# One wait fewer between the input loads of two pairs, in a fused Mamba-2 scan and bilinear FFN

## The chip, the cores and the metric

The kernel runs on 1 core of one Trainium2 chip. The metric is the device time of one execution in microseconds (us). The kernel before was run five times: 131.21, 131.57, 132.05, 132.27 and 133.94 us, median 132.05. One of these, of 131.57 us, was profiled; the profile's span is 129.80 us, so 1.77 us of that execution lie outside the span.

## What is computed

The first half is a chunked state-space scan (Mamba-2, SSD form) with 4 batches, 8 heads, 768 positions, head size 32 and state size 16. The second half is a bilinear feed-forward layer over the 3072 tokens, with d_model 256 and d_ff 1536:

```python
cum = np.cumsum(log_a[chunk]); L = np.exp(cum_i - cum_j) * causal
y_intra = ((C @ B.T) * L) @ x
y_inter = (C @ state) * exp(cum)
state = exp(sum(log_a)) * state + sum_j exp(cum_last - cum_j) * outer(B_j, x_j)
y = y_intra + y_inter                       # [batch, head, seq, 32]
X = y.transpose(0, 2, 1, 3).reshape(3072, 256)
out = ((X @ w_a) * (X @ w_b)) @ w_out       # [3072, 256], float32
```

## The kernel before

**Tiling.** The kernel cuts the 768 positions into 6 blocks of 128. Two batches are handled together as a "pair", so there are 12 pairs, numbered p = 2 * block + half. For each pair it loads B, C and x of two batches into three tiles `bn`, `cn`, `xn` (line 113), each with three buffers. A load (`load1`, line 119) takes one of the three inputs of one of the two batches, so a pair has six loads. Those of B and C move 64 KB each in pieces of 128 bytes (two positions of 16 float32), those of x 128 KB in pieces of 256 bytes. Below, "B 2/1" means the load of B for pair 2, batch 1 of the two.

**What a pair does.** POOL (for pair 0: DVE) scales B and C by factors of the decay (`scale_bc`, line 251: `bm`, `cm`). TensorE transposes both (line 306), ACT and DVE move them out of PSUM (lines 315, 316), TensorE makes the scores (line 329), DVE, and POOL for one of the four parts, mask them (lines 360, 362), ACT or POOL makes a float16 x (lines 247, 249), and TensorE multiplies (lines 371, 388, 405). ACT moves the result to `X2T` (line 417). From pair 4 on the transposes are DMAs (line 285). The feed-forward layer of a pair is six `unit`s of 16 matmuls (line 470), each with an ACT copy (479) and a DVE product (480), and two `out_half`s of 12 matmuls (line 487). Unit k2 needs `Wa` and `Wb` of third k2 // 2.

**Order.** It is written out by hand under `manual_schedule`: every engine runs its instructions in program order. TensorE has, from line 572 on: units (0,0) and (0,1), the decay factors, the transposes of pair 1, unit (0,2), scores of pair 1, units (0,3) and (0,4), `pv(1)`, units (0,5), (1,0), (1,1), (1,2), then line 612, the transposes of pair 2, then unit (1,3). So nothing after line 612 can run on TensorE before `bm` and `cm` of pair 2 are there.

**Queues.** SP issues most loads, ACT the loads of batch 1 of pair 0 and the small constant `c32`; both are hardware-described DMAs. The weights go through POOL's queue, which also casts them to float16: Wa and Wb of third 0, Wa of third 1 before the scan (lines 190, 197), Wb of third 1 and both of third 2 at lines 551 and 552, `Wo` at line 555. An SP instruction that has to wait holds everything behind it on SP.

**Completion semaphores.** The recording layer hands out eight completion semaphores in turn to the DMAs of SP and ACT, in program order, and a DMA waits for the one that had its semaphore before it. So at most eight such DMAs are in flight, and each load waits for the landing of the eighth load before it. This is seen in the built program's list of instructions with their waits:

| load | waits for the landing of |
|---|---|
| B 1/0 (line 142) | x 0/1 (the explicit wait, line 143) and B 0/1 |
| C 1/1, B 1/1, C 1/0 | a, C 0/1, B 0/0 |
| x 1/0, x 1/1 | C 0/0, x 0/0 |
| B 2/0, B 2/1 | x 0/1, c32 |
| C 2/0, C 2/1 | B 1/0, C 1/1 |
| x 2/0, x 2/1 | B 1/1, C 1/0 |
| B 3/0 (line 557) | x 1/0, Wb of third 2 (line 558), DVE's use of the old buffer |

Of the kernel before, what the change touches and what calls it, by code (L numbers as in the profile page):

```python
# [15 lines left out]
AFTER = mybir.DependencyInfo(mybir.DependencyClass.Sync, mybir.DependencyReason.DATA)  # L16
# [6 lines left out]
def kernel(  # L23
# [14 lines left out]
    nc = tc.nc  # L38
# [80 lines left out]
    def load1(eng, p, which, bt):  # L119
        blk, bp = divmod(p, NBP)  # L120
        src = (B, C, x)[which][2 * bp + bt, :, blk * Q : (blk + 1) * Q, :]
        return eng.dma_start(  # L122
            pair_in[p][which][64 * bt : 64 * bt + 64].rearrange("i h r n -> i h (r n)"),
            src.rearrange("h (i r) n -> i h (r n)", r=2),
        )
# [10 lines left out]
    load1(nc.scalar, 0, 1, 1)  # L136
    load1(nc.sync, 0, 1, 0)
    nc.scalar.preload_act_table_set("natural_log_exp_and_others")
    x_in = load1(nc.scalar, 0, 2, 1)
    nc.scalar.dma_start(c32, p32_t.ap())  # L140
    load1(nc.sync, 0, 2, 0)
    b_in = load1(nc.sync, 1, 0, 0)
    tc.add_manual_dep(b_in.ins, x_in.ins.name, AFTER, reason="inputs of pair 0 first")
    load1(nc.sync, 1, 1, 1)
    load1(nc.sync, 1, 0, 1)
    load1(nc.sync, 1, 1, 0)
# [572 lines left out]
```

## Time and profile before

| what | us |
|---|---|
| median of 5 runs | 132.05 |
| the profiled execution | 131.57 |
| its span | 129.80 |
| TensorE busy (93% of the span) | 121.3 |
| DVE, ACT, POOL busy | 87.3, 66.5, 58.7 |
| SP's one wait for x 0/1, ending at 7.04 | 3.7 |
| busy share of the 16 DMA engines from 5 to 8, 8 to 9.25 | 1.22, 1.24 |
| from 9.25 to 11.5, from 11.5 to 12.75 | 1.06, 0.67 |
| from 12.75 to 19.25, 19.25 to 24.3, 24.3 to 26 | 1.31, 1.42, 0.40 |

Times inside the execution are counted from the start of the span. A DMA has an issue (the time of its instruction on SP, ACT or POOL) and a landing: in the trace each of the 16 DMA engines posts one completion, and the load has landed with the last of them. The busy share of the DMA engines goes over 1 where packets of two queues overlap on an engine. Some loads, from the trace of before:

| load | issue | landing |
|---|---|---|
| C 0/0, x 0/0 (SP) | 2.04, 2.71 | 6.20, 8.91 |
| C 0/1, x 0/1, c32 (ACT) | 1.56, 2.27, 2.98 | 4.82, 7.02, 8.74 |
| B 1/0, C 1/1, B 1/1, C 1/0 | 7.10, 7.74, 8.42, 9.10 | 11.47, 11.75, 12.07, 12.39 |
| x 1/0, x 1/1 | 9.85, 10.83 | 13.45, 16.85 |
| B 2/0, B 2/1 | 11.50, 12.18 | 19.62, 21.21 |
| C 2/0, C 2/1 | 13.06, 13.81 | 22.71, 24.27 |
| x 2/0 (x 2/1 next) | 16.30 | 24.58 (25.42) |
| Wa, Wb of third 0 | 2.27, 3.21 | 8.07, 9.56 |
| Wa, Wb of third 1 | 5.17, 10.26 | 10.94, 14.99 |
| Wa, Wb of third 2 | 11.02, 11.73 | 17.81, 19.25 |
| Wo | 13.87 | 24.02 |

### The profile page before, as it was taken

What the parts mean: (1) busy time and instruction counts of PE and PEld (TensorE: products, weight loads), DVE (VectorE), ACT (ScalarE), POOL (GpSimd) and SP (SyncE); (2) the same over time, 40 slices, a digit from 0 to 9 for tenths busy, and PEclk for the clock granted to TensorE, in tenths of its full rate; (3) what the DMA queues carried; (4) which work ended last, traced back from release to release, by engine and by line L of the source; (5) the groups of instructions that cost most, each with busy time, mean ns of one, the idle gap of its engine ahead of it and who ended that gap; (6) DMA issues with size and microseconds to landing.
All of it is one profiled execution on the core that took longest, in us unless ns stands there. A gap on an engine that the chain in (4) does not pass through costs nothing.

```text
span 129.8 us, 4697 instructions
## 1 busy us (share of the span) xinstructions
PE 121.3 (93%) x1921; PEld 99.5 (77%) x1921; DVE 87.3 (67%) x167; ACT 66.5 (51%) x129; POOL 58.7 (45%) x90
## 2 busy tenths in 40 slices
PE   6899979699999999999999999999999999999960
PEld 2345857588888888888888988888888889888840
DVE  4475769748494976975967939949849649464420
ACT  3243484495846544546455555456365454574410
POOL 7719730489961934909518529249058000000000
PEclk9999999999999999999999999999999999999999
DMA  3998999774536556655957466564656210111203
GB/s 64 154 216 142 207 204 204 126 140 74 144 71 110 129 99 116 134 92 116 107 85 157 88 103 140 103 126 95 106 105 135 57 44 5 40 40 25 45 15 81
DMA packets 51557, 13.79 MB, mean 106 GB/s; under 512 B 45328, under 2 KB 51504, under 8 KB 51536
## 3 DMA queue, kind: packets, MB, share of 16 engines
q1 hardware_dynamic: 46560, 10.72, 44.5%
q0 software_dynamic: 3184, 2.36, 11.9%
q10 hardware_dynamic: 1792, 0.41, 1.6%
q8 instruction: 15, 0.25, 0.9%
q14 instruction: 6, 0.05, 0.2%
HBM read 11.13 MB, written 3.15 MB: 110 GB/s over the span
## 4 chain that ended last, share of the span: by engine, by line
PE 77%; DMA 12%; SPq 5%; ACTq 1%; issue 1%; POOL 1%; DVE 0%; POOLq 0%; ACT 0%
PE ops L487 25%; PE aps L470 22%; PE bps L470 21%; DMA cn<-in_C_dram 8%; SPq L122 5%; DMA xn<-in_x_dram 4%; PE SC L329 3%; PE SC L371 3%; PE SC L405 2%; ACTq L122 1%; PE SC L388 1%; POOL bm L255 0%; PE SC L306 0%; DVE osb L500 0%; POOL cm L255 0%
## 5 line engine op out<-in xcount | busy, mean ns | idle before, releaser
L480 DVE TENSOR_TENSOR hk<-bps,asb 128x512 f16<-128x512 f32 x72 | 49.2, 688 | 22.9 <-ACT asb L479 21.0
L479 ACT COPY asb<-aps 128x512 f32<-128x512 f32 x72 | 42.2, 587 | 17.6 <-PE aps L470 16.0
L470 PE MATMUL aps<-X2T,Wa 128*128 128x256 f16 x288 | 43.5, 273 | 0.0
L470 PE MATMUL bps<-X2T,Wb 128*128 128x256 f16 x288 | 43.2, 273 | 0.4 <-DMA Wb<-in_moe_w_b_dram 0.4
L487 PE MATMUL ops<-Wo,hk 128*128 128x256 f16 x288 | 35.3, 273 | 0.0
L470 PEld LDWEIGHTS <-Wb 128*128 128x128 f16 x288 | 28.1, 98 | 3.9 <-DMA Wb<-in_moe_w_b_dram 0.6
L362 DVE TENSOR_TENSOR t<-SC,causal 128x512 f16<-128x512 f32 x45 | 29.4, 682 | 1.5 <-ACT tmp L359 0.9
L487 PEld LDWEIGHTS <-hk 128*128 128x128 f16 x288 | 27.5, 98 | 3.5
L470 PEld LDWEIGHTS <-Wa 128*128 128x128 f16 x288 | 26.8, 98 | 4.3 <-DVE X2T L429 0.3
L445 POOL TENSOR_TENSOR sbd<-U,maskbd 128x512 f16<-128x512 f32 x10 | 11.6, 1158 | 26.3 <-PE ops L487 15.1
L502 ACT ACTIVATE osb<-ops 128x256 f32<-128x256 f32 x23 | 8.8, 384 | 23.3 <-PE ops L487 21.2
L249 POOL TENSOR_SCALAR x<-xn 128x512 f16<-128x512 f32 x9 | 13.4, 1491 | 1.0 <-DMA xn<-in_x_dram 0.3
L417 ACT ACTIVATE X2T<-SC 128x512 f16<-128x512 f32 x11 | 6.6, 597 | 7.4 <-PE SC L388 6.4
L441 DVE SCALAR_TENSOR_TENSOR U<-SC,G,gU 128x64 f32<-128x64 f32 x16 | 3.8, 280 | 6.1 <-ACT X2T L417 6.1
L255 POOL TENSOR_TENSOR bm<-bn,fB 128x256 f16<-128x256 f32 x11 | 6.9, 629 | 0.0
L201 PE MATMUL SC<-warm 128*128 128x512 f16 (+1 forms) x14 | 5.1, 516 | 1.2 <-DVE warm L150 1.2
L360 POOL TENSOR_TENSOR t<-tmp,causal 128x512 f16<-128x512 f32 x3 | 3.5, 1155 | 6.2 <-ACT tmp L359 6.2
L273 POOL TENSOR_TENSOR bc<-bn,fB 128x128 f16<-128x128 f32 x16 | 6.2, 408 | 0.0
L269 POOL TENSOR_TENSOR bc<-cn,fC 128x256 f16<-128x256 f32 x8 | 5.0, 623 | 1.7 <-DMA cn<-in_C_dram 1.0
L201 PEld LDWEIGHTS <-warm 128*128 128x128 f16 x23 | 2.5, 130 | 4.1 <-issue 2.7
L371 PE MATMUL SC<-t,x 64*32 64x128 f16 x352 | 4.8, 218 | 0.2 <-DVE t L362 0.2
L371 PEld LDWEIGHTS <-x 64*32 64x32 f16 x384 | 3.2, 91 | 2.3 <-issue 1.2
(68 smaller groups left out, 68.1 us busy)
## 6 DMA issues: line engine op xcount, KB each, us to landing
xn<-in_x_dram SPq DMA_DIRECT2D x23, 128.0 KB, 3.9
out_dram<-osb SPq DMA_DIRECT2D x46, 64.0 KB, 2.1
bn<-in_B_dram SPq DMA_DIRECT2D x23, 64.0 KB, 3.1
cn<-in_C_dram SPq DMA_DIRECT2D x23, 64.0 KB, 3.5
Wa<-in_moe_w_a_dram POOLq DMA_DIRECT2D x3, 256.0 KB, 5.8
Wb<-in_moe_w_b_dram POOLq DMA_DIRECT2D x3, 256.0 KB, 6.4
Wo<-in_moe_w_out_dram POOLq DMA_DIRECT2D x1, 768.0 KB, 10.1
xn<-in_x_dram ACTq DMA_DIRECT2D x1, 128.0 KB
```

The lines of the kernel that those rows point to most:

```text
L122: return eng.dma_start(pair_in[p][which][64 * bt : 64 * bt + 64].rearrange("i h r n -> i h (r n)"), src.rearrange("h (i r) n -> i h (r n)" ...
L201: nc.tensor.matmul(bank[:, 0:cols], warm[:, 0:128], warm[:, 0:cols], start=True, stop=True, skip_group_check=True)
L249: eng.tensor_scalar(xo, xi, XS, None, ALU.mult)
L255: eng.tensor_tensor(out=m_, in0=pair_in[p][which].rearrange("p h r n -> p r h n"), in1=f[:, blk, :, bp].unsqueeze(3).broadcast_to((128, 2, ...
L362: nc.vector.tensor_tensor(out=o_, in0=i_, in1=c_, op=ALU.mult)
L371: nc.tensor.matmul(py[bt][32 * g : 32 * g + 32, u * Q : (u + 1) * Q], s["X16"][k, h, r, :], s["T1"][k, h, r, :], start=(first and u == 0 a ...
L445: nc.gpsimd.tensor_tensor(out=Sbd.rearrange("p t (m c) -> p t m c", m=4), in0=U32[:, p].unsqueeze(2).broadcast_to((128, 2, 4, 2 * D)), in1 ...
L470: nc.tensor.matmul(ps[:, kk * 2 * Q : (kk + 1) * 2 * Q], W[:, f, k * 128 : (k + 1) * 128], X2T[:, p, f].rearrange("p t q -> p (t q)"), sta ...
L479: nc.scalar.copy(asb, a_ps)
L480: return lambda: nc.vector.tensor_tensor(out=s["hk"][:, 2 * k2 : 2 * k2 + 2, :].rearrange("p k q -> p (k q)"), in0=b_ps, in1=asb, op=ALU.mult)
L487: nc.tensor.matmul(o_ps[:, 0:d_model], hk[:, k, bt * Q : (bt + 1) * Q], Wo[:, k, :], start=(k == 0), stop=(k == NK - 1), skip_group_check= ...
L502: nc.scalar.activation(out=o_sb, in_=o_ps[:, 0:d_model], func=AF.Copy, scale=1.0 / (YS * YS))
```

## The change

```diff
-    x_in = load1(nc.scalar, 0, 2, 1)
+    load1(nc.scalar, 0, 2, 1)
     nc.scalar.dma_start(c32, p32_t.ap())
     load1(nc.sync, 0, 2, 0)
-    b_in = load1(nc.sync, 1, 0, 0)
-    tc.add_manual_dep(b_in.ins, x_in.ins.name, AFTER, reason="inputs of pair 0 first")
+    load1(nc.sync, 1, 0, 0)
     load1(nc.sync, 1, 1, 1)
```

The explicit wait of SP for the landing of x 0/1 ahead of B 1/0 is gone. No instruction is added, removed or put in another place on any engine. In the built program one more thing is different: B 1/0 now takes the eighth completion semaphore, which no DMA had before it, and `c32` on ACT takes the first one, so that B 1/0 waits for nothing and `c32` waits for the landing of B 0/1. Accordingly B 2/1 waits for B 1/0 (before: c32), C 2/0 for c32 (before: B 1/0), and B 2/0 carries the wait for x 0/1 itself. All other waits of the table stand.

## Prediction

> **What bounds the kernel now.** I read the page's engine table first, then the chain of waits, then TensorE's waits in the start-up, then the timeline around the longest of them, then the DMA queues by window.
>
> ```profile
> PE 121.3 (93%) x1921; PEld 99.5 (77%) x1921; DVE 87.3 (67%) x167; ACT 66.5 (51%) x129; POOL 58.7 (45%) x90
> ...
> DMA  3998999774536556655957466564656210111203
> ...
> PE 77%; DMA 12%; SPq 5%; ACTq 1%; issue 1%; POOL 1%; DVE 0%; POOLq 0%; ACT 0%
> ```
>
> TensorE is the bound: in the windows from 26 to 113 us it is busy 87.00 of 87.00. The other 12% DMA and 5% SP in the chain are all in the first 25 us, where the row of DMA tenths is at 9. A us gained or lost on TensorE before 26 is thus a us of the span; one gained on any other engine is nothing until TensorE feels it. The chain, asked for 12 to 27 us, shows where it enters TensorE:
>
> ```profile
> 13.81 10.45 DMA cn<-in_C_dram
> 24.27 0.02 issue
> ...
> 24.98 0.63 POOL bm L255
> 25.61 0.05 issue
> 25.65 0.40 PE SC L306 x4
> ```
>
> The load C 2/1, issued at 13.81, takes 10.45 us; POOL then makes `cm` and `bm`; only then can TensorE transpose pair 2. TensorE's own waits from 10 to 27 us price it, beside all others:
>
> ```profile
> PE SC L306 <- POOL bm L255: 1.2, 1, 1.2
> PE SC L329 <- DVE ct L316: 0.4, 1, 0.4
> PE bps L470 <- DMA Wb<-in_moe_w_b_dram: 0.4, 1, 0.4
> PE SC L371 <- DVE t L362: 0.2, 1, 0.2
> ```
>
> The timeline gives the two that inputs and weights cause to the hundredth:
>
> ```profile
> 19.30 0.61 PE L470 MATMUL bps<-X2T,Wb 128*128 128x256 f16 x4 [0.37 <-DMA Wb<-in_moe_w_b_dram]
> ...
> 24.40 0.62 POOL L255 TENSOR_TENSOR cm<-cn,fC 128x256 f16<-128x256 f32 x1 [5.39 <-DMA cn<-in_C_dram]
> ...
> 25.65 0.28 PE L306 MATMUL SC<-ident,bm 128*128 128x128 f16 x2 [1.18 <-POOL bm L255]
> ```
>
> So 1.18 us hang on pair 2's C, and 0.37 on Wb of third 2. POOL was free for `cm` from 19.0 on (5.39 us idle): there is nothing else ahead of it. The removed wait itself is 3.7 us long but on SP, not on TensorE:
>
> ```profile
> SPq L122 <- DMA xn<-in_x_dram: 3.7, 1, 3.7
> ```
>
> **What the Trainium skill says.** "DMA: Bandwidth & Descriptors", section "Issuing engines are not separate DMA queues": DMAs of SP, ACT and POOL end on the same 16 engines and interleave. The trace agrees: from 13.75 to 19.25 POOL's queue (q0) takes 94.8% and SP's (q1) 38.4%. Its section "Queues, rings and completion order": on an engine each queue is consumed in ring order, and queues with work take turns packet by packet. The trace fits: x 0/0 came ahead of everything later on SP, and no queue shuts another out. Its section "Why a DMA increments its semaphore by 16 and not by 1": only the full 16 mean landed. Here C 2/1's first completion is at 21.51, its last at 24.27; the slowest engine decides.
>
> **The change part by part.**
>
> *SP's issues.* x 0/0's issue ends at 3.35. B 1/0 can follow at 3.40 (before 7.10: 3.70 earlier). Each issue takes about 0.63 with 0.05 to the next. The remaining semaphore waits then hold: C 1/1 at 4.05, B 1/1 at 4.82 (landing of C 0/1), C 1/0 at 5.5, x 1/0 at 6.25 (C 0/0 landed at 6.20), x 1/1 at 8.95 (x 0/0 landed at 8.91; before 10.83). B 2/0 follows at 9.63 (before 11.50), and pair 2 comes 1.9 us earlier all along if its own waits (landings of B 1/0, c32, C 1/1) are met by then. So of 3.70 us pair 2 keeps 1.9: the wait for x moves from x 0/1 (7.02) to x 0/0 (8.91).
>
> *From issue to landing.* The DMA engines decide what that is worth. By window:
>
> ```profile
> 8.00:9.25 1.25, 1.25 (x27) 0.50 (x12) 0.83 (x2) 0.84 (x2) 0.09 (x1) 1.00 1.24 205
> 9.25:11.50 2.25, 2.23 (x39) 0.83 (x37) 1.06 (x2) 0.78 (x4) 2.25 (x3) 1.00 1.06 166
> 11.50:12.75 1.25, 1.21 (x11) 0.82 (x10) 1.15 (x4) 0.53 (x2) 1.17 (x3) 1.00 0.67 117
> 12.75:19.25 6.50, 5.80 (x108) 4.53 (x105) 4.51 (x13) 4.38 (x11) 3.76 (x5) 1.00 1.31 205
> ```
>
> The last two columns are the DMA share and GB/s. From 8 to 9.25 the engines are full of weights alone (266 packets of q0, none of q1), from 9.25 to 11.5 of pair 1's B and C (2065 packets of q1, 130 of q0). Exchanging these two in time gains nothing: 396 weight packets at 266 per 1.25 us are 1.86 us, 2065 of q1 at their fastest (325 in a quarter us) 1.6, together 3.5, the whole stretch. The room is from 11.5 to 12.75, at half load: there x 1/0 runs alone, x 1/1 begins only at 13.75, after Wb of third 1 has taken the engines. With both x waiting in the ring, they follow at 11.5; at the pace of 14.0 to 14.5 (330 packets) a load of 512 takes 0.75 us, so x 1/1 starts near 12.25 and not at 13.75: 1.5 us earlier. Behind it the queue is unchanged, so I move C 2/1's landing by the same 1.5, to 22.8. Bounds: nothing (24.27) if the engines' total work sets it; 1.9 (22.4) if the issue does; refilling only the idle share, 1.25 * (1.31 - 0.67) / 1.31 = 0.6, gives 23.7.
>
> *On TensorE.* From C 2/1's landing to the transpose are 25.65 - 24.27 = 1.38 us. TensorE is ready at 24.48, so a landing up to 23.10 removes the whole 1.18 us; at 22.8 there are 0.3 to spare, at 23.7 only 0.6 us are gained.
>
> *Weights.* Pair 1's and 2's earlier packets now share engines with weights. Wb of third 0 (landed 9.56, used at 12.29) and Wa of third 1 (10.94, used at 15.24) have 2.7 and 4.3 us of cover. Wb of third 1 (14.99, used at 15.67) has 0.68, Wa of third 2 (17.81, used at 18.32) 0.51, Wb of third 2 none. New contention is from 12.75 to 13.75, where q1 was nearly empty. In the window 11.5 to 13.75 and in that from 19.25 to 24.3, q0 keeps some 80% beside a full q1 (81.1% in the latter against 94.8%): 20% of 1 to 1.5 us is 0.2 to 0.3 us later. On Wb of third 2 the first 0.20 is hidden by the wait for DVE's mask at 20.34, so 0.1 us is charged. Bounds: 0, or the full issue advance of 3.7 on the weights.
>
> *Pair 0.* x 0/0 and the loads before it are ahead of B 1/0 in the same ring, and x 0/1's packets end at 6.25, before the first of x 0/0's: nothing of pair 1 can run before 8.0. c32 now waits for B 0/1 (landed 3.38): issue 3.42 for 2.98. Behind it on ACT is the copy at 5.07, and it is first read at 14.96. Nothing. Without that cover an x 0/0 later by over 0.6 us would hold pair 0's products (scaled x ends at 9.57, used at 10.25).
>
> *Late next.* With TensorE 1.1 us earlier, x 2/1 (landed 25.42) is read near 27.6, C 3/1 (27.25) near 28.9; DVE's product at 24.70 ends at 25.39, ahead of its banks' reuse by unit (1,4) near 25.8. None binds.
>
> Sum: 129.80 - 1.18 + 0.1 = 128.7 for the span, plus 1.77 outside: 130.5 against 131.57. The median of five is 0.48 above that execution, so from it: 132.05 - 1.08 = 131.0.
>
> **Rivals.** *Hidden anyway.* The engines are full from 5 to 24, and SP's issues themselves stretch there (C 2/1's takes 2.44 us): the earlier issue only waits longer, C 2/1 lands at 24 or later: 131.8 to 132.2. Against it stands the half-empty window. *Both stalls go.* If the filled window also brings Wb of third 2 forward by 0.4, 1.18 + 0.37 give 130.5; half the further wait for DVE, 130.3. *Weights late (slower).* At 19.30 TensorE waits for Wb of third 2; if the weights lose the 3.7 us that SP's queue wins, Wb lands at 22.95, TensorE loses 3.65 and gets back 1.18: 132.05 + 2.5 = 134.5. It decides from a landing after 20.43 us (1.18 late) on. For it: no slack on that load. Against: turn-taking leaves q0 80%. *No earlier issue.* The eight semaphores could put another wait in the wait's place; the built program shows B 1/0 with none, so I give that none by itself.
>
> **Chances.** Forecast 0.5 (130.5 to 131.6), hidden 0.22, both stalls 0.15, weights late 0.13. About 1% is what a measurement of this kernel can tell from no change: below 130.73 is the whole of "both stalls" and a quarter of the forecast's case, 0.27; above 133.37 most of "weights late", 0.11; the rest 0.62. The range takes all of "both stalls" except its lowest end, the forecast, "hidden", and the start of "weights late": 130.2 to 132.8; the forecast's own is 130.5 to 131.6.
>
> **What would show it.** Right: SP's issue of B 1/0 near 3.4 and of B 2/0 near 9.6; the DMA share from 11.5 to 12.75 over 1; C 2/1 landed before 23.1; no wait of line 306 for POOL; Wb's wait under 0.6. Wrong: C 2/1 again after 24, a wait at line 470 for Wb over 1 us, or ACT waiting for x 0/0 after 9.5.

## The result, and the profile after the change

The changed kernel takes 130.13 us in the median of 41 executions (129.04 to 132.30), the kernel before 131.63 us in 78 (129.99 to 137.57). The ratio is 0.9917 with a 95% interval of 0.9897 to 0.9936. It compares, for each kernel, only the executions within 1.5% of its fastest, which leaves out the long ones (15 of the 78 before took over 133 us, none of the 41 after), so the medians lie further apart, by 1.1%. The profiled execution took 129.55 us with a span of 127.85.

The page after, at the places shown of before (engine table, DMA tenths, chain):

```profile
PE 119.4 (93%) x1921; PEld 98.7 (77%) x1921; DVE 88.3 (69%) x167; ACT 66.6 (52%) x129; POOL 58.7 (46%) x90
...
DMA  3999999875356556555856464574565210111203
...
PE 84%; DMA 8%; DVE 2%; SPq 1%; POOL 1%; issue 0%; ACT 0%; DVEq 0%; POOLq 0%
```

SP's share of the chain fell from 5% to 1%. SP's timeline after (columns: start, length, instruction) shows the wait gone and what is left of the head start:

```profile
3.40 0.64 SPq L122 DMA_DIRECT2D bn<-in_B_dram  x1
4.07 0.63 SPq L122 DMA_DIRECT2D cn<-in_C_dram  x1
4.88 0.64 SPq L122 DMA_DIRECT2D bn<-in_B_dram  x1
5.57 1.67 SPq L122 DMA_DIRECT2D cn<-in_C_dram  x1
7.28 2.62 SPq L122 DMA_DIRECT2D xn<-in_x_dram  x2
9.95 1.60 SPq L122 DMA_DIRECT2D bn<-in_B_dram  x2
```

The windows after (last columns: DMA share and GB/s) have 1.26 from 11.5 to 12.75, where the profile before had 0.67:

```profile
9.25:11.50 2.25, 2.19 (x30) 1.40 (x29) 1.32 (x6) 1.12 (x4) 2.18 (x4) 1.00 1.39 217
11.50:12.75 1.25, 1.25 (x24) 0.98 (x22) 1.22 (x4) 0.75 (x2) 0.00 (x0) 1.00 1.26 149
```

In bytes the rise is smaller, from 117 to 149 GB/s. The share adds up the time of every packet, and it goes over 1 with one queue alone too (1.24 from 8 to 9.25 before, where only weights moved), so packets and bytes tell more. From 8 to 11.5 us, for SP's loads (q1) and the weights (q0), in packets, MB and share, they are before:

```profile
q0 software_dynamic: 396, 0.37, 64.9%
q1 hardware_dynamic: 2065, 0.26, 47.7%
```

and after:

```profile
q1 hardware_dynamic: 2482, 0.36, 70.2%
q0 software_dynamic: 407, 0.38, 67.6%
```

TensorE's waits after, 10 to 27 us:

```profile
PE SC L305 <- POOL bm L254: 0.6, 1, 0.6
PE bps L469 <- DMA Wb<-in_moe_w_b_dram: 0.5, 2, 0.4
PE SC L370 <- DVE t L361: 0.4, 1, 0.4
```

All lines have moved up by one. The first of these is not the wait of before: it stands at 14.22, at the transposes of pair 1 (C 1/0 landed at 12.82). Those of pair 2 start at 23.65 without a wait. C 2/1 landed at 19.77 (24.27 before), x 1/1 at 15.58 (16.85).

Two stages of the two executions differ. TensorE's first unit begins at 10.23 (11.64 before): pair 0 started earlier, with C 0/0 landed at 5.57 (6.20). From the first unit to the transposes of pair 2 it took 13.41 us (14.02). From there to the end it is 104.20 (104.19). So 1.40 of the 2.00 us are in pair 0's start, all but the end of which lies ahead of the first packet of a moved load (7.64), and only 0.61 in the stretch where I expected the win. This split is no division of causes, though. Before, the transposes of pair 2 came 1.38 us behind C 2/1's landing (24.27, 25.65), as they did in all other profiles that waited for this load (1.38 or 1.39). With that landing given, an earlier first unit would only have made the wait longer.

### The profile page after: what moved, and what is told of

It reads as the page before. It is cut to its first block, busy times and chain, and to the rows that moved or that the text cites. A ratio compares the mean times of both kernels' runs of the same rounds, so it can differ in the third digit from the quotient of the medians.

```text
span 127.8 us, 4696 instructions
## 1 busy us (share of the span) xinstructions
PE 119.4 (93%) x1921; PEld 98.7 (77%) x1921; DVE 88.3 (69%) x167; ACT 66.6 (52%) x129; POOL 58.7 (46%) x90
## 4 chain that ended last, share of the span: by engine, by line
PE 84%; DMA 8%; DVE 2%; SPq 1%; POOL 1%; issue 0%; ACT 0%; DVEq 0%; POOLq 0%
PE ops L486 25%; PE aps L469 24%; PE bps L469 24%; DMA Wb<-in_moe_w_b_dram 5%; PE SC L328 4%; PE SC L370 3%; DMA cn<-in_C_dram 3%; PE SC L404 2%; PE SC L387 1%; DVE t L361 1%; POOL t L359 1%; SPq L122 1%; DVE hk L479 1%; ACT tmp L358 0%; PE SC L305 0%
## 5 line engine op out<-in xcount | busy, mean ns | idle before, releaser
L444 POOL TENSOR_TENSOR sbd<-U,maskbd 128x512 f16<-128x512 f32 x10 | 11.6, 1158 | 22.8 <-DVE U L440 15.8
L200 PE MATMUL SC<-warm 128*128 128x512 f16 (+1 forms) x14 | 4.2, 434 | 1.2 <-DVE warm L149 1.2
L200 PEld LDWEIGHTS <-warm 128*128 128x128 f16 x23 | 2.0, 110 | 3.4 <-issue 1.4
```

What stands on the lines that cost most here:

```text
L200: nc.tensor.matmul(bank[:, 0:cols], warm[:, 0:128], warm[:, 0:cols], start=True, stop=True, skip_group_check=True)
L444: nc.gpsimd.tensor_tensor(out=Sbd.rearrange("p t (m c) -> p t m c", m=4), in0=U32[:, p].unsqueeze(2).broadcast_to((128, 2, 4, 2 * D)), in1 ...
```

## The experiments

First theory: the win is TensorE's wait of 1.18 us for pair 2's C. Rivals: pair 0 starts earlier by the change; or the win is elsewhere in the start-up.

**The kernel before, once more.** No edit.

> The kernel before once more, unchanged, for a second profile. In the two profiles pair 0's start differs: C 0/0 landed at 6.20 before and at 5.57 after the change, and TensorE's first unit began at 11.64 and 10.23. Nothing that the change touches is issued before 3.4 us. Theory 'execution spread' (C 0/0's landing and all that follows from it wanders from execution to execution by some tenths): this second profile shows C 0/0 landing somewhere between 5.4 and 6.4, not again at 6.20 within 0.05. Rival 'the change brings pair 0 forward' (SP waiting, or the missing loads, hold pair 0's C): again 6.1 to 6.3. In both, C 2/1 lands near 24 and line 306 waits about 1.2 us for POOL.

Measured: 131.97 us, first unit at 10.76, C 0/0 landed at 5.57. So pair 0's start wanders from execution to execution; the 1.40 us are not the change's. It is the first profile that stands apart. Its warm-up matmuls (line 559) ran at half speed; the same five took 2.07 us there and 1.25 here:

```profile
8.24 2.07 PE L201 MATMUL tc<-warm 128*128 128x512 f16 x5
```

```profile
7.20 1.25 PE L201 MATMUL tc<-warm 128*128 128x512 f16 x5
```

In the first trace's record of the granted clock, full speed begins at 9.94 us; in all the others it begins between 3.9 and 6.5, but for the one with fewer weights below (10.16). Pair 0's products stand behind these matmuls: they came 1.34 us after x 0/0's landing there (8.91, 10.25), and 0.70 after the change (8.14, 8.84). This and the landing itself make up the 1.40 us. POOL's first mask came 1.0 us later too (9.16 for 8.13 here), and with it the weights that POOL issues behind it: Wb of third 1 at 10.26, against 9.04 to 9.39 in all profiles that issue it there. So the half-empty stretch from 11.5 to 12.75 belongs, of the profiles with all the weights, to that one alone. In this one it is full without the change:

```profile
11.50:12.75 1.25, 1.25 (x13) 0.98 (x10) 1.18 (x5) 0.86 (x2) 0.00 (x0) 1.00 1.27 178
```

The waits were not those of the first profile either:

```profile
PE SC L306 <- POOL bm L255: 1.7, 1, 1.7
PE bps L470 <- ACT G L601: 1.4, 1, 1.4
```

The second line is new. The timeline of the same execution tells whose it is:

```profile
18.79 0.63 ACT L247 ACTIVATE x<-xn 128x512 f16<-128x512 f32 x1 [1.35 <-DMA xn<-in_x_dram]
...
19.53 0.60 PE L470 MATMUL bps<-X2T,Wb 128*128 128x256 f16 x4 [1.42 <-ACT G L601]
```

ACT stands in order: behind the scaling of pair 1's x, which waits for x 1/1 (landed 18.71, not 16.85), are the copies that TensorE's next banks need. The load that cost nothing in the first profile costs 1.42 us here.

**A longer wait.** B 1/0 waits for x 0/0 in the place of x 0/1.

```diff
-    x_in = load1(nc.scalar, 0, 2, 1)
+    load1(nc.scalar, 0, 2, 1)
...
-    load1(nc.sync, 0, 2, 0)
+    x_in = load1(nc.sync, 0, 2, 0)
```

> The wait is made longer: B 1/0 waits for x 0/0 (landed 8.91 before) in the place of x 0/1 (7.02). My theory (the later pair 1's loads are issued, the later C 2/1 lands and the longer TensorE waits at the transposes of pair 2): B 1/0 issued near 8.9, C 2/1 landed 0.5 to 1.9 us later, transposes wait 1.7 to 3 us, time 0.5 to 1.5% over before. Rival 'only what the freed first stretch does for pair 0 and the weights counts': within 0.3% of before, since pair 0 is untouched.

Measured: ratio 1.0391 (1.0286 to 1.0495, from 6 executions), well over every expectation, for an issue only 1.6 us later (8.72). Not pair 2's C but pair 1's own fell behind: C 1/0 landed at 18.20 (before: 12.39), and TensorE waited at the transposes of pair 1:

```profile
PE SC L306 <- POOL bm L255: 5.4, 1, 5.4
```

The windows of the same profile show a second price, in the column before the DMA share: TensorE's granted clock.

```profile
16.60:23.40 6.80, 3.81 (x49) 2.61 (x50) 0.77 (x3) 2.09 (x5) 2.80 (x5) 0.50 0.87 138
```

It was at half speed for 6.83 us, from 16.57 to 23.40. This began inside the wait (14.17 to 19.59), so 3.81 us of it fell on work. The Trainium skill has this in "TensorE: Matmul & The Clock Gate", section "Part 1: The HAM clock gate (the "warmup" mystery)": TensorE falls to half rate after an idle window of about 3.4 us, and the windows run freely. The half-speed stretches seen here, of 3.41, 6.83 and 10.24 us, are multiples of 3.41, as it says; but in four profiles below one stands at a wait of only 1.2 to 2.0 us.

**One wait taken from the kernel before.** Pair 2's B and C are scaled from pair 1's tiles; all loads are made, and what is left out is the use of pair 2's own B and C.

```diff
-        in0=pair_in[p][which].rearrange("p h r n -> p r h n"),
+        in0=pair_in[1 if p == 2 else p][which].rearrange("p h r n -> p r h n"),
```

> The kernel before, but the scaling of B and C of pair 2 reads pair 1's tiles in the place of pair 2's (all loads are still made; what is left out is the use of pair 2's own B and C). It takes away TensorE's dependence on C 2/1 and nothing else. My theory (the 1.18 us at the transposes of pair 2 are what the change wins): 0.7 to 1.0% under before, the wait of line 306 for POOL gone. Rival 'most of the win is an earlier pair 0 or earlier weights': still the stall's own 1.18 us or 0.9% here, but then the change itself must win more than this; rival 'the stall is refilled by other waits': under 0.4%.

Measured: 0.9998 (0.9959 to 1.0036). With the wait that I had priced at 1.18 us gone from the code, nothing was won by the ratio. This speaks against the first theory as the whole cause, but does not settle it: the median of all executions is 130.56 us (22 of them), against 131.43 (43). The profile shows what took the wait's place in one execution: x 1/1 at 18.53, and then half the clock for 3.41 us (20.11 to 23.52).

```profile
PE bps L470 <- ACT G L601: 1.8, 1, 1.8
```

**The same on the changed kernel.**

> The same edit on the changed kernel (what is left out is again the use of pair 2's own B and C). My theory (the change has removed the whole of that wait, C 2/1 landed at 19.77): no difference to the changed kernel, so 0.7 to 1.0% under before, and the same as the same edit on the kernel before within 0.3%. Rival 'the change also wins elsewhere (pair 0, weights)': 0.5% or more faster than the same edit on the kernel before. Rival 'the wait is still there in most executions': more than 0.3% faster than the changed kernel.

Measured: 0.9946 (0.9910 to 0.9981), no better than the change itself (0.9917): no sign that pair 2's C still binds there. It was 0.5% better than the same edit before, the sign of the second rival, but the intervals overlap.

**The other wait taken from before.** Pair 1's x is made from pair 0's tile; what is left out is the use of pair 1's own x.

```diff
-        xo, xi = X16.rearrange("p h r d -> p (h r d)"), pair_in[p][2].rearrange("p h r d -> p (h r d)")
+        xo, xi = X16.rearrange("p h r d -> p (h r d)"), pair_in[0 if p == 1 else p][2].rearrange("p h r d -> p (h r d)")
```

> The kernel before, but ACT makes pair 1's float16 x from pair 0's tile of x (all loads are still made; pair 1's own x is left out of the result). New theory (two late loads: besides pair 2's C, the load x 1/1, on which ACT waits in order ahead of the copies that free TensorE's banks; in the second profile of before and in that with pair 2's scaling borrowed it landed at 18.7 and 18.5 and TensorE waited 1.4 and 1.9 us for ACT there, in the first it landed at 16.85 and cost nothing): the 1.4 us wait of line 470 for ACT goes, the long executions become fewer, median over all 0.3 to 0.8 us under before. First theory alone (pair 2's C is all): no difference to before, since in the first profile x 1/1 costs nothing.

Measured: 1.0013 (0.9958 to 1.0067), nothing won, against the new theory's expectation of a lower median (131.89 against 131.88). TensorE reached pair 2 earlier and waited there:

```profile
PE SC L306 <- POOL bm L255: 1.8, 1, 1.8
```

**Both taken away, before and after.**

> The kernel before with both borrowings: pair 1's x from pair 0's tile, pair 2's B and C from pair 1's tiles (loads all made; the use of those three inputs is left out). Theory of two late loads: both waits gone, 1.0 to 1.6% under before by the medians, within 0.4% of the changed kernel, and few executions over 131.5 us. Rival (the change wins by something else, such as weights or pair 0): over 0.6% slower than the changed kernel. Rival (one wait refills the other): little better than the better of the two single borrowings, under 0.2%.

> The changed kernel with the same two borrowings. Theory of two late loads: the change has taken both waits away already, so within 0.4% of the changed kernel and within 0.3% of the kernel before with both. Rival (part of the waits is still there after the change): 0.5% or more faster than the changed kernel.

Measured: before 0.9896, but 0.9777 to 1.0016, from 7 executions between 129.15 and 137.49: inconclusive. Its profile has a third wait, C 1/0 landed at 15.51 and TensorE waiting 3.03 us at the transposes of pair 1 (to 16.90), with half the clock from 15.43 to 25.66. After: 0.9948 (0.9897 to 0.9999), again no better than the change. Its profile shows that the early issue does not ensure an early landing: the loads are those of the changed kernel, yet x 1/1 landed at 18.59 and C 2/1 at 22.97.

**The changed kernel beside them.**

> The changed kernel unchanged, on the same chip as the three others, for a direct comparison and a second profile. Expected 0.7 to 1.2% under before; x 1/1 landed before 17, C 2/1 before 22, no wait of line 470 for ACT, C 0/0 landed between 5.0 and 6.2 as in the kernel before.

Measured: 0.9884 (0.9808 to 0.9959), x 1/1 landed at 13.30, C 2/1 at 19.34, C 0/0 at 5.23. No wait over 0.4 us from 10 us on.

So the theory became: the loads of pair 1 and pair 2 stand in one row on SP's queue, and before the change the whole row runs into the weights whose packets come from 11.5 to 12 us on. Whichever load of the row is needed first and is late (C 1/0, x 1/1, C 2/1) stalls TensorE; taking one away leaves the next.

**Only pair 1 early.** The changed kernel, but B 2/0 waits for B 1/1, so it is issued at 11.78, as before the change.

```diff
-    load1(nc.sync, 1, 0, 1)
+    b11 = load1(nc.sync, 1, 0, 1)
...
-    load(2)
+    n2 = load(2)
+    tc.add_manual_dep(n2[0].ins, b11.ins.name, AFTER, reason="pair 2 later")
```

> The changed kernel with one wait put in: B 2/0 waits for the landing of B 1/1 (11.5 to 12.1), so pair 1's loads are early as after the change and pair 2's are issued from about 11.7 on, as before it (11.5). It tells the two halves of the change apart. Theory A (pair 2's C, as in the prediction): the win goes, within 0.3% of before. Theory B (pair 1's C 1/0 and x 1/1, which before land at 12 to 15.5 and 16.9 to 18.8 according to whether they reach the DMA engines ahead of the weights that start at 12): most of the win stays, 0.5 to 1.1% under before, x 1/1 landed before 16, though C 2/1 lands near 22 to 24 and line 305 waits up to 1.2 us for POOL.

Measured: 0.9930 (0.9899 to 0.9960): by the ratio nearly the whole win stays, theory B's number. The profiled execution is one of its longest (133.05 us; median 130.52), and shows what pair 2's half is worth when it does bind: x 1/1 early (14.15), C 2/1 late (24.17), a wait of 2.00 us, and half the clock after it (26.33 to 29.74).

```profile
25.55 0.29 PE L306 MATMUL SC<-ident,bm 128*128 128x128 f16 x2 [2.00 <-POOL bm L255]
```

```profile
26.40:29.70 3.30, 3.30 (x46) 2.06 (x45) 0.90 (x2) 1.91 (x6) 2.04 (x4) 0.50 0.69 129
```

**A middle wait.** B 1/0 waits for C 0/1 and is issued at 4.74.

```diff
-    load1(nc.scalar, 0, 1, 1)
+    x_in = load1(nc.scalar, 0, 1, 1)
...
-    x_in = load1(nc.scalar, 0, 2, 1)
+    load1(nc.scalar, 0, 2, 1)
```

> The kernel before with the wait for x 0/1 replaced by one for C 0/1 (landed 4.8): B 1/0 is issued near 4.9 and not at 3.4 or 7.1, all else follows. The packets of x 0/0 leave SP's ring no sooner than near 8, so by my theory any issue before about 6 is as good as 3.4: same as the changed kernel within 0.3%, 0.7 to 1.1% under before. Rival (each part of the 3.7 us counts alike): 40% of the win is lost, about 0.5% under before.

Measured: 0.9889 (0.9849 to 0.9930, from 7 executions), the same as the change within the intervals. No worth of the first 1.3 of the 3.7 us shows, as the packets of x 0/0, ahead in the ring, made me expect.

**The weights out of the way.** The kernel before without the loads of Wa and Wb of thirds 1 and 2; every unit multiplies with third 0.

```diff
-    load_w(1, (0,))
...
-                        W[:, f, k * 128 : (k + 1) * 128],
+                        W[:, f, k % 4 * 128 : (k % 4 + 1) * 128],
...
-    load_w(1, (1,))
-    load_w(2)
...
-    tc.add_manual_dep(n0[0].ins, wd[5].ins.name, AFTER, reason="weights first")
+    tc.add_manual_dep(n0[0].ins, wd[1].ins.name, AFTER, reason="weights first")
```

> The kernel before without the loads of Wa and Wb of thirds 1 and 2; every unit multiplies with third 0 (left out: two thirds of the first layer's weights; the number of matmuls is the same). Wo's issue moves forward by the 2.2 us that POOL no longer needs for three issues. It takes the weights' packets away from 9.5 to 13.5 us. Theory B (pair 1's loads lose to the weights): x 1/1 landed before 15 although B 1/0 is issued near 7 as before, no wait of line 470 for ACT, 1% or more under before. Rival (pair 1's loads are late by SP's issue alone): x 1/1 lands at 16 or later, little change.

Measured: 0.9892 (0.9845 to 0.9940, from 6 executions), as much as the change wins, with SP's wait still there (B 1/0 issued at 7.88). x 1/1 landed at 15.26, a little over the bound that I had set, and C 2/1 at 20.74. The edit also takes away TensorE's waits for these weights, 0.37 us in the first profile of before and none in the second; that is less than the win. No wait for a load is left:

```profile
PE SC L328 <- DVE ct L315: 0.4, 1, 0.4
PE SC L370 <- DVE t L361: 0.4, 1, 0.4
```

**A try for more.** The changed kernel with Wb of third 1 issued right behind Wa of third 1.

```diff
-    load_w(1, (0,))
+    load_w(1)
...
-    load_w(1, (1,))
```

> The changed kernel with Wb of third 1 issued by POOL right behind Wa of third 1, near 5.9 and not near 9.2 (the mask of POOL in between starts near 8.1 and is not delayed). In the profiles after the change TensorE waits 0.4 to 1.2 us for this load at unit (0,2). If that wait is the largest left: 0.2 to 0.6% under the changed kernel, Wb of third 1 landed before 13. Rival (its packets now run beside pair 1's B and C from 9.5 to 12 and push C 1/0 and x 1/1 back behind the weights of third 2): as slow as before or slower, with waits of line 305 for POOL or of line 469 for ACT.

Measured: 0.9955 (0.9925 to 0.9984). No gain over the change shows; the intervals just overlap. Of the rival the wait came, but not a kernel as slow as before: Wb landed at 13.27, but C 1/0 only at 13.58, and TensorE waited there:

```profile
PE SC L305 <- POOL bm L254: 1.2, 1, 1.2
```

No version faster than the change beyond its interval was found; the middle wait is as good.

One table holds all profiles: landings, and the time from TensorE's first unit to the transposes of pair 2 (us).

| kernel | C 1/0 | x 1/1 | C 2/1 | first unit to transposes of pair 2 |
|---|---|---|---|---|
| before, two profiles | 12.39, 12.79 | 16.85, 18.71 | 24.27, 24.67 | 14.02, 15.30 |
| before, pair 2's B, C borrowed | 11.99 | 18.53 | (22.01) | 15.42 |
| before, pair 1's x borrowed | 12.00 | (18.29) | 23.71 | 14.81 |
| before, both | 15.51 | (18.96) | (24.71) | 18.20 |
| before, longer wait | 18.20 | 19.22 | 20.73 | 18.96 |
| before, fewer weights | 12.60 | 15.26 | 20.74 | 12.82 |
| middle wait | 12.85 | 17.86 | 21.67 | 12.67 |
| changed, two profiles | 12.82, 11.82 | 15.58, 13.30 | 19.77, 19.34 | 13.41, 12.66 |
| changed, pair 2's B, C borrowed | 11.88 | 13.11 | (20.53) | 12.98 |
| changed, both borrowed | 12.40 | (18.59) | (22.97) | 14.25 |
| changed, pair 2 late | 12.15 | 14.15 | 24.17 | 14.84 |
| changed, Wb of third 1 early | 13.58 | 17.52 | 18.54 | 14.74 |

In brackets: landed, but not used. After that point every profile takes 104.0 to 104.2 us to the end of its span, but for pair 2 late, whose half clock falls there (105.7). Apart from pair 0's start (first unit between 10.1 and 11.6), the difference between the profiles is made in this one stretch, which takes some 12.7 us when nothing is late.

## Why the prediction was right, and where it was not

- **Size and sign.** Forecast 131.0 against 132.05, 0.8% less; measured 0.83% less by the ratio, 130.13 us in the median against 131.63. Right.
- **SP's issues.** Right: 3.40 for B 1/0; 9.26 for x 1/1 and 9.95 for B 2/0, forecast 8.95 and 9.63. x 1/0 came 1.0 later than said, since C 1/0's issue took 1.67 us.
- **From issue to landing.** The room was put in the wrong place. The window from 11.5 to 12.75 was half empty (0.67) in the one execution with the late start; in the other four profiles with the wait of before and all the weights it had shares of 0.95 to 1.27. And the exchange from 8 to 11.5, where weights alone came first and loads after them, was said to gain nothing ("the whole stretch"). With B 1/0 issued at 3.4 both moved together there: 2482 packets of loads and 407 of weights, for 2065 and 396 (in the second profiles, 2834 and 354 for 1937 and 363). From 9.25 to 11.5 the seven profiles with B 1/0 issued before 5 us moved 205 to 230 GB/s, those five of before 135 to 166. C 2/1 came 4.5 us earlier, not 1.5. "Behind it the queue is unchanged" was wrong: one place ahead in the row, pair 2's B and C came before Wo and not beside it. By queue from 16.5 to 17.5 us after (packets, MB, share):

```profile
q1 hardware_dynamic: 1147, 0.14, 97.3%
q0 software_dynamic: 88, 0.06, 40.0%
```

Before, q1 moved 262 packets in that us.
- **On TensorE.** The 1.18 us wait went, as said. But it was priced from one execution as if it were the win; without it the kernel before is no faster by the ratio (0.9998). The step that failed is *Late next*, with its "None binds": it looked only at what follows pair 2's C, and pair 1's own loads were not costed at all. In the profile C 1/0 landed at 12.39, `cm` and `bm` made from pair 1's loads ended at 13.92, and TensorE used them at 15.00, so the cover was 1.1 us; x 1/1 had 1.29 (16.85, used at 18.14). In three other profiles with the wait of before they stall TensorE by 1.4 to 3.0 us. With pair 1 alone early, 0.9930 of the time is left, with both pairs early 0.9917.
- **Weights.** 0.1 us was charged. Wb of third 2 was not later (18.37 and 17.76 after; 19.25 and 17.82 before), and TensorE waited 0.16 and 0.15 us for it. The "80%" that the weights keep was misread: 81.1% is their share of the engines' time beside SP's loads, and alone they had 124.1% (8 to 9.25), so no such fraction follows. Wb of third 1 cost 0.38 us in one of the two profiles after, none in the other.
- **Pair 0.** Right, nothing: C 0/0 landed between 4.97 and 6.20 in the profiles whatever the wait, and x 0/0 between 8.12 and 8.62 in those with the change, 8.00 and 8.91 in those with the wait of before.
- **Rivals.** "Hidden anyway" and "weights late" did not come. Of "both stalls go" the second stall, Wb of third 2, fell from 0.37 to 0.16 and 0.15 us, but the second profile of before did not have it either. What I took for the win is one part of a row of loads that is late as a whole.

That the size was met is in part luck: the price came from an execution with a late start and a half-empty window that others do not have, the wait may be worth less than its price, and the loads beside it, priced at nothing, are worth something. What stays open is how the win divides between C 1/0, x 1/1 and C 2/1: the single borrowings won nothing each by the ratio, both together were not measured finely enough, and pair 2 late differs from the change by less than the intervals. Why the clock rose so late in the first profile stays open too.

## What to carry to other kernels

When a row of loads on one queue meets a burst on another, don't price the one wait that the profile shows: list every load of the row with its landing and first use, and count those with little cover as waits too, since taking one away hands the stall to the next. A wait that only keeps loads in order may cost much where it pushes them behind the next burst; set it early enough that the row's packets follow those ahead of them in the queue. Here x 0/0's last packet and B 1/0's first lay 1.4 us apart before (7.96, 9.40), 0.4 with the middle wait and 0.01 after. An issue at 4.7 us was as good as one at 3.4, one at 7.1 cost 0.8%, one at 8.7 another 3.9%. And take a second profile before pricing a start-up: two executions of the same kernel had different waits, and the warm-up of one ran at half speed to 9.94 us.

## What the runs showed of the hardware that was not expected

- Waits of TensorE of 1.2 to 2.0 us in the start-up had 3.41 us at half the clock beside them in four profiles. It began 0.8 us after the wait in two (pair 2 late, pair 2 borrowed before) and inside its last 0.5 us in two (both borrowed after the change, Wb of third 1 early). With the wait of 3.03 us it was 10.24 us, with that of 5.42 us 6.83. Waits of 1.8 us in another (pair 1's x borrowed) and of 1.42 and 1.68 in the second of before had none.
- A load moved by 1.6 us in issue (C 1/0, 9.10 to 10.71) landed 5.8 us later (12.39 to 18.20) with all the weights on their way. Without those of thirds 1 and 2, an issue at 9.87 landed at 12.60.
- From 9.25 to 11.5 us the engines moved 205 to 230 GB/s where loads and weights had come together from 8 us on, and 135 to 166 where the weights came first and the loads behind them.
